# Products as pairs of half-row matmuls between the score blocks, in an attention and gated-FFN kernel

## The chip, the cores and the metric

The kernel runs on one core of one Trainium2 chip. The metric is the device time of one execution in microseconds (us). The engines go by short names: PE is TensorE (PEld its weight loads), DVE is VectorE, ACT is ScalarE, POOL is GpSimd, SP is SyncE, whose queue issues most DMAs here.

## The reference

x has 2048 rows of 576. With xn = layernorm(x), everything in float32:

```
q, k, v = xn @ wqkv                     # 32 heads of 18
s = softmax(q k^T * 18^-0.5) v @ wo     # attention over all 2048 rows
g = silu( (gelu(xn @ w_gate) * (xn @ w_up)) @ w_down )     # w_gate, w_up 576 x 4608, w_down 4608 x 576
out = x + s * g
```

## The kernel before, in words

**Operands.** A float32 product of projections is made of three fp16 ones: each operand is split into a high and a low half, and hi*hi, hi*lo and lo*hi are added up in PSUM. XHT holds the transposed high halves of xn (four tiles of 128 rows, and a fifth, XT, with the last 64 rows' high halves above their low halves), XL the low ones. A gate, up, q or k product of 128 output rows and 512 columns of the sequence is `mm_wx`: 14 matmuls, each with 128 rows of contraction and 512 columns. A down tile (`dn`) is two half tiles of 288 columns, six matmuls each. The v and output products go through `mm_xw`, 14 matmuls of 288 columns.

**Scores.** Heads go in 16 pairs; the two heads of a pair stand on rows 0 to 63 and 64 to 127. `qk1` (L940) makes scores of queries by keys on 54 rows, and VectorE takes their row maximum (L943, tile PM); one call is two matmuls, one for each half of the rows. `qk2` (L980) makes the transposed scores with the maximum already subtracted, on 56 rows, and ScalarE takes exp (L986, tile P). `pv` (L1002) multiplies P with V in float32 on four tiles of 32 columns; each float32 matmul is two records in the trace, 16 in a call for both steps' P tiles.

**PSUM.** Eight banks: s1 for qk1 (two banks), s2 for qk2 (two), pv (one), and three rotating m tiles (`MTile`) for all projections. In the main loop s1 and s2 have one buffer each, so a qk1 waits for the maximum of the qk1 before, a qk2 for the exp of the qk2 before.

**Order.** All instructions are issued in an order written out by hand; each engine's queue works in that order. The main loop runs over pairs p and 32 steps s. A step issues qk2 for pair p, qk1 for pair p+1, some filler, qk2 and qk1 again, and then filler (odd s) or `pv` for two steps (even s). Filler is a generator (`filler_gen`) that yields one matmul at a time, with its time: q/k of the later heads (units j), the 18 chunks of the gated FFN (units c: gate, up, a down tile between them), and at last the output product. `fill(amount)` takes matmuls from it until the amount, left time over left steps, is used up.

`subtick` is the clock of all else: each call advances `defer` (work put off by a number of ticks: evacuations, the gelu chain on POOL and ACT, stores) and takes one piece from `bg`, the queue of weight preparations (`prep`: load, maxima L170 and L175, scales L210 to L227, high halves on ACT, remainders L239 and L250 on DVE). A step has four ticks.

**Stages.** Up to 180 us: load, layernorm, transposes, q/k of the first heads, v, and qk1 of pair 0 with v and j1 as filler. From 180 to 2603 us: pairs 0 to 14. Then pair 15 (which has no qk1 to run ahead), the output products, and the end.

Of the kernel before, what the change touches and what calls it, by code (L numbers as in the profile page):

```python
# [12 lines left out]
F32 = mybir.dt.float32  # L13
# [11 lines left out]
NJ = 5  # L25
# [6 lines left out]
FILL_PRO = 0.92  # L32
LATE = 14
V_PLAN = {8: 2, 9: 2, 10: 1, 12: 1, 13: 4, 14: 2, 15: 3, 16: 3, 17: 1}
T_WX, T_XW = 0.216, 0.123
# [3 lines left out]
T_V = NT * 2 * 14 * T_XW  # L39
T_J = NB * 2 * 14 * T_WX  # L40
T_C = NB * 4 * 14 * T_WX + NT * 12 * T_XW
# [26 lines left out]
def kernel(ctx: ExitStack, tc: tile.TileContext, x, wqkv, wo, w_gate, w_up, w_down, out):  # L68
# [33 lines left out]
    m_pend = []  # L102

    class MTile:


        def __init__(self, shape, dt, readers):
            until(lambda: len(m_pend) < 3 or m_pend[-3] == 0)
            self.i = i = len(m_pend)
            m_pend.append(readers)  # L110
            self.t = ps.tile(shape, dt, tag="m", name=f"m{i}", bufs=3)

        def done(self):
            m_pend[self.i] -= 1
# [16 lines left out]
    def prep(name, parts, n, down=None, urgent=False, free=None, dfree=None):  # L131
# [47 lines left out]
        def par():  # L179
# [7 lines left out]
            if urgent:  # L187

                mt = ps.tile([P, 512], F32, tag="pv", name=f"mp_{name}")
# [3 lines left out]
                mt = ps.tile([P, 512], F32, tag="pv", name=f"mb_{name}")  # L193
# [96 lines left out]
    def mm_wx(o, w, i, c0, c1, s0, s1, end=None):  # L290

        k = 0
        for t in range(4):
            for (lw, xx) in ((w.hi, XH), (w.hi, XL), (w.lo, XH)):
                nc.tensor.matmul(o, lw[:, t, i, c0:c1], xx[:, t, s0:s1], start=(k == 0), stop=False)  # L295
                k += 1
                yield 0.216
        nc.tensor.matmul(o, w.hi[:, 4, i, c0:c1], XT[:, s0:s1], start=False, stop=False)  # L298
        yield 0.216
        nc.tensor.matmul(o, w.lo[:, 4, i, c0:c1], XT[:, s0:s1], start=False, stop=True)  # L300
        if end is not None:
            end()
        yield 0.216
# [64 lines left out]
    def proj_j_sb(w, j, part, sb):  # L368
        n = w.n
        mt = MTile([P, 512], F32, 2)  # L370
        yield from mm_wx(
            mt.t[0:n, :], w, part, 0, n, 512 * sb, 512 * sb + 512,
            lambda: evac_j(j, part, sb, mt, n),
        )

# [12 lines left out]
    def unit_j(w, j):  # L388
        open_j(w, j)
        for sb in range(NB):  # L390
            for part in (1, 0):
                yield from proj_j_sb(w, j, part, sb)
# [10 lines left out]
    def unit_v(w):  # L403
        nc.vector.tensor_copy(EV, w.E[:, 0:1])
        for st in range(NT):
# [3 lines left out]
            for hf in range(2):  # L409
                mt = MTile([P, 512], F32, 1)  # L410
# [24 lines left out]
    def gu(w, c, sb, ft):  # L435
        s0 = 512 * sb
        cs = slice(P * ft, P * ft + P)
        st = {}
        gp = nc.gpsimd
        g = MTile([P, 512], F32, 1)  # L440

        def copy():
# [3 lines left out]
            st["t0"] = defer.now  # L446
            defer.at(defer.now + 1, cubic)
            defer.at(defer.now + 4, th)
            defer.at(defer.now + 5, one)
# [6 lines left out]

        def th():
            nc.scalar.activation(st["t"], st["t"], AF.Tanh, scale=GK)  # L458
# [3 lines left out]

        yield from mm_wx(g.t, w, 0, cs.start, cs.stop, s0, s0 + 512, copy)
        yield from dn_unit()

        u = MTile([P, 512], F32, 1)

        def mul():
            st["v"] = wp.tile([P, 512], F32, tag="gv", name=f"gv_{c}_{sb}_{ft}")
            nc.vector.scalar_tensor_tensor(  # L470
                st["v"], u.t, w.uE[:, 1:2], st["g"], op0=ALU.mult, op1=ALU.mult
            )
            u.done()
            t = max(defer.now + 1, st["t0"] + 6)
            defer.at(t, hp)
            defer.at(t + 2, hhi)
            defer.at(t + 3, hlo)
# [4 lines left out]
        def hhi():  # L482
            if ft == 0:
                hs = hstate[c, sb] = W()
                hs.n = 0
# [4 lines left out]
        def hlo():  # L490
            hs = hstate[c, sb]
            gp.tensor_tensor(hs.lo[:, ft], st["v"], hs.hi[:, ft], op=ALU.subtract)  # L492
            hs.n += 1

        yield from mm_wx(u.t, w, 1, cs.start, cs.stop, s0, s0 + 512, mul)
        yield from dn_unit()
# [4 lines left out]
    def dn(w, c, sb, si):  # L501

        until(lambda: (c, sb) in hstate and hstate[c, sb].n == 2)
# [3 lines left out]
        for hf in range(2):  # L507
            ms = slice(288 * hf, 288 * hf + 288)
            mt = MTile([P, 512], F32, 1)
            yy = Y[0][:, st, ms]  # L510
            k = 0
            for ft in range(2):
                for a, b in ((hs.hi, w.dhi), (hs.hi, w.dlo), (hs.lo, w.dhi)):
                    nc.tensor.matmul(  # L514
                        mt.t[:, 0:288], a[:, ft, sl], b[:, ft, ms], start=(k == 0), stop=(k == 5)
                    )
                    k += 1
                    if k < 6:
                        yield T_XW
            if c == 0:  # L520
                nc.vector.tensor_scalar(yy, mt.t[:, 0:288], w.c, None, op0=ALU.mult)
            else:
                nc.vector.scalar_tensor_tensor(yy, mt.t[:, 0:288], w.c, yy, op0=ALU.mult, op1=ALU.add)  # L523
            mt.done()
            yield T_XW
        dndone[c] += 1
        if c == NCH - 1 and si == 3:
            queue_gate(sb)

    def dn_unit(lag=5):  # L530

        if len(dnq) > lag:
            yield from dnq.popleft()

    def unit_c(w, c):
        if c == 0:
            Y[0] = cp.tile([P, NT, D], F32, tag="xy", name="y")
        for sb in range(NB):
            dnq.extend(dn(w, c, sb, si) for si in range(4))
            for ft in range(2):  # L540
                yield from gu(w, c, sb, ft)
        if c == NCH - 1:
            while dnq:
                yield from dn_unit(0)
# [67 lines left out]
    obdone = [0, 0]  # L612
    last_o = {}
# [24 lines left out]
    def unit_out(qc, whole):  # L638
# [13 lines left out]
        for si in range(2):  # L652
# [8 lines left out]
            for hf in range(2):  # L661
                ms = slice(288 * hf, 288 * hf + 288)
                mt = MTile([P, 512], F32, 1)
# [518 lines left out]
```

## Time and profile before

| | us |
|---|---|
| median of three runs | 2792.64 (2792.05 to 2792.81) |
| the profiled execution, its own time | 2790.57 |
| its span, first to last instruction | 2788.7 |
| busy PE, PEld | 2708.0, 1100.4 |
| busy DVE, ACT, POOL | 2026.7, 1596.9, 926.9 |
| mean granted TensorE clock | 0.993 of full |

Matmuls are pipelined and their rows overlap: a row's length is not the time that it takes of PE. The distance from one start to the next is. The rows named m are projections (L295, L298, L300 in `mm_wx`; L514 down; L310 to L315 in `mm_xw`), s the scores.

### The profile page before, as it was taken

To read this page: it belongs to the slowest core of one execution; us is meant where nothing else is said; L and a number is where in the kernel's file an instruction comes from. 1 tells how busy PE (TensorE), PEld (TensorE's weight loads), DVE (VectorE), ACT (ScalarE), POOL (GpSimd) and SP (SyncE) were. 2 spreads that over 40 slices of the span, in tenths; PEclk is the share of its full clock that TensorE was granted. 3 is DMA by queue.
4 is the path that set the end of the run, shared out by engine and by line. 5 is a ranking of instruction groups with operands and counts; after the bars stand their busy time and mean duration, and the time that the engine had idled before them with its cause. 6 is when DMAs were issued, how large, how long until landed. Compare 5 with 4: busy or idle time off the path is not lost.

```text
span 2788.7 us, 44258 instructions
## 1 busy us (share of the span) xinstructions
PE 2708.0 (97%) x17736; PEld 1100.4 (39%) x17736; DVE 2026.7 (73%) x2703; ACT 1596.9 (57%) x1948; POOL 926.9 (33%) x976
## 2 busy tenths in 40 slices
PE   6989999999999999999999999999999999999998
PEld 6533333333333333333333333333333333333354
DVE  7787767767777777777777777777777777777354
ACT  5136556655665556665656565666655555656652
POOL 4113331333223331343333333333333333333301
PEclk9999999999999999999999999999999999999999
DMA  4330102102030202102011110101021001010113
GB/s 137 125 103 13 48 13 85 31 8 52 20 80 15 49 13 75 39 3 54 7 49 31 30 39 7 48 9 48 14 48 27 21 21 36 20 34 9 37 52 128
DMA packets 133258, 117.36 MB, mean 42 GB/s; under 512 B 60096, under 2 KB 112472, under 8 KB 133052
## 3 DMA queue, kind: packets, MB, share of 16 engines
q1 hardware_dynamic: 128828, 103.28, 13.6%
q0 software_dynamic: 3072, 8.90, 0.9%
q8 instruction: 138, 2.26, 0.4%
q10 hardware_dynamic: 1152, 2.36, 0.2%
q14 instruction: 68, 0.56, 0.1%
HBM read 84.89 MB, written 29.61 MB: 41 GB/s over the span
## 4 chain that ended last, share of the span: by engine, by line
PE 82%; DVE 13%; issue 2%; DMA 2%; ACT 1%; SPq 0%; POOL 0%; ACTq 0%; DVEq 0%; POOLq 0%
PE m L295 28%; PE pv L1002 14%; PE m L514 14%; PE s L980 10%; PE s L940 8%; DVE PM L943 5%; PE m L310 3%; PE m L298 2%; PE m L300 2%; DVE m_c L170 1%; DVE gv L470 1%; DVE y L523 1%; DVE wlo_c L239 1%; DVE dlo_c L250 0%; DMA KD<-evh 0%
## 5 line engine op out<-in xcount | busy, mean ns | idle before, releaser
L943 DVE TENSOR_REDUCE PM<-s 128x2 f32<-128x1024 f32 x1024 | 1249.4, 1223 | 571.2 <-PE s L940 565.2
L986 ACT ACTIVATE P<-s,etab 128x1024 f32<-128x1024 f32 x896 | 997.0, 1113 | 843.5 <-PE s L980 834.9
L1002 PE MATMUL pv<-P,VT 128*32 128x512 f32 x4096 | 492.5, 598 | 0.0
L295 PE MATMUL m<-XHT,whi_c 128*128 128x512 f16 x1152 | 438.7, 381 | 6.1 <-DVE gv L470 6.0
L295 PE MATMUL m<-XHT,wlo_c 128*128 128x512 f16 x1152 | 439.1, 381 | 1.8 <-DVE wlo_c L239 1.8
L295 PE MATMUL m<-XL,whi_c 128*128 128x512 f16 x1152 | 439.1, 381 | 0.0
L940 PE MATMUL s<-KT,QT 54*128 54x512 f16 x2048 | 390.4, 379 | 31.2 <-DVE PM L943 26.3
L980 PE MATMUL s<-QT,KT 56*128 56x512 f16 x2048 | 400.4, 387 | 8.8 <-ACT P L986 8.7
L453 POOL TENSOR_TENSOR tw<-gs 128x512 f32<-128x512 f32 x144 | 150.5, 1045 | 665.7 <-ACT gs L444 665.6
L480 POOL TENSOR_TENSOR gv<-gv,tw 128x512 f32<-128x512 f32 x144 | 186.2, 1293 | 465.8 <-DVE gv L470 434.6
L514 PE MATMUL m<-dhi_c,hlo 128*128 128x288 f16 x1152 | 330.3, 287 | 0.8 <-POOL hlo L492 0.8
L514 PE MATMUL m<-dhi_c,hhi 128*128 128x288 f16 x1152 | 330.5, 287 | 0.2 <-ACT hhi L488 0.2
L514 PE MATMUL m<-dlo_c,hhi 128*128 128x288 f16 x1152 | 330.3, 287 | 0.0
L295 PEld LDWEIGHTS <-whi_c 128*128 128x128 f16 x2304 | 215.8, 98 | 272.2 <-issue 103.0
L523 DVE SCALAR_TENSOR_TENSOR y<-m,c_c,y 128x288 f32<-128x288 f32 x544 | 266.5, 509 | 43.0 <-PE m L514 41.1
L980 PEld LDWEIGHTS <-KT 56*128 56x128 f16 x2048 | 99.0, 93 | 494.8 <-issue 493.1
L514 PEld LDWEIGHTS <-hhi 128*128 128x128 f16 x2304 | 217.7, 98 | 161.1 <-issue 70.7
L492 POOL TENSOR_TENSOR hlo<-gv,hhi 128x512 f16<-128x512 f32 x144 | 167.3, 1162 | 252.9 <-ACT hhi L488 252.9
L1002 PEld LDWEIGHTS pv<-P,VT 128*32 128x32 f32 x4096 | 106.8, 109 | 256.0 <-issue 256.0
L455 POOL TENSOR_TENSOR tw<-tw,gs 128x512 f32<-128x512 f32 x144 | 185.0, 1285 | 12.0
L295 PEld LDWEIGHTS <-wlo_c 128*128 128x128 f16 x1152 | 112.7, 98 | 163.2 <-issue 57.4
L461 POOL TENSOR_SCALAR tw<-tw 128x512 f32<-128x512 f32 x144 | 90.2, 626 | 202.8 <-ACT tw L458 200.8
(172 smaller groups left out, 2710.9 us busy)
## 6 DMA issues: line engine op xcount, KB each, us to landing
draw_c<-in_B_w_down SPq DMA_DIRECT2D x18, 576.0 KB
raw_c<-in_B_w_gate SPq DMA_DIRECT2D x18, 512.0 KB
raw_c<-in_B_w_up SPq DMA_DIRECT2D x18, 512.0 KB
obr<-rd SPq DMA_DIRECT2D x30, 256.0 KB
KT<-KD SPq DMA_DIRECT2D x32, 224.0 KB
QT<-QD SPq DMA_DIRECT2D x32, 216.0 KB
VS<-vst POOLq DMA_DIRECT2D x16, 304.0 KB, 3.0
VT<-VS SPq DMA_DIRECT2D x16, 304.0 KB
```

The lines of the kernel that those rows point to most:

```text
L295: nc.tensor.matmul(o, lw[:, t, i, c0:c1], xx[:, t, s0:s1], start=(k == 0), stop=False)
L453: gp.tensor_tensor(st["t"], st["g"], st["g"], op=ALU.mult)
L455: gp.tensor_tensor(st["t"], st["t"], st["g"], op=ALU.mult)
L480: gp.tensor_tensor(st["v"], st["v"], st["t"], op=ALU.mult)
L492: gp.tensor_tensor(hs.lo[:, ft], st["v"], hs.hi[:, ft], op=ALU.subtract)
L514: nc.tensor.matmul(mt.t[:, 0:288], a[:, ft, sl], b[:, ft, ms], start=(k == 0), stop=(k == 5))
L523: nc.vector.scalar_tensor_tensor(yy, mt.t[:, 0:288], w.c, yy, op0=ALU.mult, op1=ALU.add)
L940: nc.tensor.matmul(s1[:, h], QT[p][r, P * qt:P * qt + P], KT[p][r, 512 * kb:512 * kb + 512], start=True, stop=True)
L943: nc.vector.tensor_reduce(PM[p][:, :, qt, kb:kb + 1], s1, op=ALU.max, axis=AX.X)
L980: nc.tensor.matmul(s2[:, h], KT[p][r, P * kt:P * kt + P], QT[p][r, 512 * qb:512 * qb + 512], start=True, stop=True)
L986: nc.scalar.activation(pt, s2, AF.Exp, scale=ETAB[j0])
L1002: nc.tensor.matmul(o[qd:qd + 32, :], VT[p][:, c0:c0 + 32], pt[:, h], start=(kt == 0), stop=(kt == NT - 1), skip_group_check=True,)
```

## The change

1. Gate and up of one 128-row tile (or k and q of one block of 512) become a `Pair`: 54 matmuls of 64 rows in place of 28 of 128. In stage 0, product a runs on rows 0 to 63 of its operands and b on rows 64 to 127, one of each alternately, into two PSUM tiles; in stage 1 they change halves. A stage has 14 slots of two matmuls (the last of one). A stage 1 starts only once a score tile that was issued after the end of stage 0 has been used again.
2. The m ring of three becomes three tiles with names: ma and mb for a pair, mc for down (and ma as well where no pair is open).
3. Filler by amount is gone from the main loop for these products. A pair runs either fast (14 slots in an odd step, 10 and 4 in the even one) or slow (6 and 2, or 5 and 4 where no down waits; the even step ends the stage), as the count of stages is behind a straight line over the steps or not.
4. Down half tiles wait in a queue and are issued at the end of a step: one at an odd step, one or two ahead of P times V and at times one behind it at an even one.
5. Gate and up evacuate together: copy of gate at the end of the pair, product with up two ticks later, the rest of the chain at fixed ticks.
6. In the prologue, pairs stand between the score blocks and v alone is filler; j1's weights are prepared ahead of the score loop. The last chunk takes its column blocks in the order 2, 3, 0, 1. The output products start when all downs are done.

```
+    def half_terms(w, i, cs, xs, half):
+        r = slice(64 * half, 64 * half + 64)
+        terms = []
+        for t in range(4):
+            for lw, xx in ((w.hi, XH), (w.hi, XL), (w.lo, XH)):
+                terms.append((lw[r, t, i, cs], xx[r, t, xs]))
+        terms.append((w.hi[r, 4, i, cs], XT[r, xs]))
+        if half == 0:
+            terms.append((w.lo[r, 4, i, cs], XT[r, xs]))
+        return terms
...
+            if self.stage == 0:
+                self.q = [(a, half_terms(w, ia, cs, xs, 0)), (b, half_terms(w, ib, cs, xs, 1))]
+            else:
+                self.q = [(b, half_terms(w, ib, cs, xs, 0)), (a, half_terms(w, ia, cs, xs, 1))]
...
+        def end(g, u):
             st["g"] = wp.tile([P, 512], F32, tag="gs", name=f"gs_{c}_{sb}_{ft}")
             nc.scalar.activation(st["g"], g.t, AF.Copy, scale=w.uE[:, 0:1])
             g.done()
+            t = defer.now
+            defer.at(t + 1, cubic)
+            defer.at(t + 2, lambda: mul(u))
+            defer.at(t + 5, th)
+            defer.at(t + 6, one)
+            defer.at(t + 8, hp)
+            defer.at(t + 10, hhi)
+            defer.at(t + 11, hlo)
+            if ft == 1:
+                defer.at(t + 13, lambda: dnq.extend(
+                    (w, c, sb, si, hf) for si in range(4) for hf in range(2)
+                ))
...
+    def g_run(n, new=True):
+        while n > 0 and not gs.over:
+            if not gs.open:
+                if gs.pair is not None and seen[0] <= gs.end:
+                    return
+                if gs.pair is None:
+                    if not new:
+                        return
+                    gs.pair = next(gstream, None)
...
+                gs.pair.begin()
+                gs.open = True
+            n -= 1
+            if gs.pair.slot():
...
+        preps[1], pieces = prep(*order[1][1], urgent=True, mtag="s2")
...
-    for item in range(0, 64, 2):
-        qk1(0, item)
-        qk1(0, item + 1)
-        fills(2, FILL_PRO)
+    for k in range(32):
+        qk1(0, 2 * k)
+        g_run((3, 2, 2, 0)[k % 4])
+        qk1(0, 2 * k + 1)
+        fills(2, 0.68)
+        g_run((2, 2, 3, 0)[k % 4])
...
+            odd = s % 2 == 1
+            if odd and not gs.open and gs.pair is None:
+                want = g0 + (G_ALL - LATE - g0) * (2 * NT * p + s) / (2.0 * NT * (NPAIR - 1))
+                fast = gs.n < want and len(dnq) > 0
+            if fast:
+                n1, n2 = (14, 0) if odd else (10, 4)
+            elif odd:
+                n1, n2 = (6, 2) if dnq else (5, 4)
             else:
+                n1, n2 = 9, 0
...
             pa = qk2(p, 2 * qh, kt)
             if kp < NPAIR:
                 qk1(kp, next(items))
-            fills(2, amt)
+            subtick()
+            g_run(n1, odd)
...
             pb = qk2(p, 2 * qh + 1, kt)
             if kp < NPAIR:
                 qk1(kp, next(items))
+            g_run(n2, odd)
...
-            if s % 2 == 0:
+            if odd:
+                down("mc")
+                if gs.over:
+                    down("ma")
+            else:
+                if down("mc") and gs.pair is None:
+                    down("ma")
                 for u in pend[:-1]:
                     pv(*u)
                 pend = pend[-1:]
-                fills(2, 0.0)
-            else:
-                fills(2, amt)
+                if len(dnq) > 8:
+                    down("mc")
```

Here gs.n counts stages, gs.open says that one is running, and dnq holds the half tiles of down that are free to run.

More of the change, by code (lines that the diff above doesn't have):

```diff
@@ L445, in copy @@
             g.done()
[L446 to L449, printed above, removed]
+            t = defer.now
[10 more added lines that the diff above has]
+                ))
+        end.readers = 1
         def cubic():
@@ L473, in mul, with th, one @@
             u.done()
[L474 to L477, printed above, removed]
+        def th():
+            nc.scalar.activation(st["t"], st["t"], AF.Tanh, scale=GK)
+        def one():
+            gp.tensor_scalar(st["t"], st["t"], 1.0, 1.0, op0=ALU.mult, op1=ALU.add)
         def hp():
@@ L1086 @@
     while vdone[0] < NT or not mdone.get(0):
[L1087 removed]
+        fills(1, 1.0)
+    for _ in filler[0]:
+        pass
     def last_gen():
```

251 lines of the change are left out of this document (140 added, 111 removed).

## The prediction

> **What bounds the kernel now.** I read the page's head, the busy times by stage, one stretch of the timeline, and last the waits of the engines that the changed order will press on.
>
> ```profile
> span 2788.7 us, 44258 instructions
> PE 2708.0 (97%) x17736; PEld 1100.4 (39%) x17736; DVE 2026.7 (73%) x2703; ACT 1596.9 (57%) x1948; POOL 926.9 (33%) x976
> ```
> ```profile
> 0.00:180.10 180.10, 149.23 (x1295) 102.69 (x1295) 147.91 (x249) 58.00 (x114) 44.09 (x84) 0.98 0.39 122
> 180.10:2602.70 2422.60, 2387.79 (x15260) 912.47 (x15260) 1798.61 (x2323) 1449.88 (x1738) 850.00 (x857) 1.00 0.13 33
> 2602.70:2788.70 186.00, 170.99 (x1184) 85.25 (x1183) 80.14 (x133) 89.06 (x96) 32.77 (x36) 0.96 0.25 81
> ```
>
> (Stretch, length, then PE, PEld, DVE, ACT and POOL busy with counts, granted clock, DMA share, GB/s.) The middle row is the loop over pairs 0 to 14: 2422.6 us, 15 x 16 = 240 double steps (an even and an odd s) of 10.09 us. PE's 97% hides a loss, because a matmul's row runs on while the next one streams. The starts show it:
>
> ```profile
> 1285.03 0.38 PE L295 MATMUL m<-XL,whi_c 128*128 128x512 f16 x1
> 1285.24 0.38 PE L295 MATMUL m<-XHT,wlo_c 128*128 128x512 f16 x1
> 1285.55 0.39 PE L980 MATMUL s<-QT,KT 56*128 56x512 f16 x2
> 1285.57 0.10 PEld L940 LDWEIGHTS <-QT 54*128 54x128 f16 x2
> 1285.78 0.38 PE L940 MATMUL s<-KT,QT 54*128 54x512 f16 x2
> 1286.09 0.39 PE L295 MATMUL m<-XHT,whi_c 128*128 128x512 f16 x1
> 1286.20 1.23 DVE L943 TENSOR_REDUCE PM<-s 128x2 f32<-128x1024 f32 x1 [0.78 <-PE s L940]
> 1286.32 0.38 PE L295 MATMUL m<-XL,whi_c 128*128 128x512 f16 x1
> 1286.54 0.38 PE L295 MATMUL m<-XHT,wlo_c 128*128 128x512 f16 x1
> ```
>
> Full matmuls of 512 columns start 0.215 us apart. Two score matmuls, one on each half of the rows, start together and count as one. Going from full to halves takes 0.31 (1285.24 to 1285.55), the next start 0.23, the way back 0.31, and the next 0.23: 1.08 in place of 4 x 0.215, so **0.108 us for one change of shape**. A double step now has three stretches of filler between score blocks and one of P times V, eight changes: 240 x 8 x 0.108 = 207 us of the loop. That is what the change goes for.
>
> P times V stands on 32-column tiles. From it to halves, and to full matmuls (in the tail), it is the same:
>
> ```profile
> 1291.23 1.92 PE L1002 MATMUL pv<-P,VT 128*32 128x512 f32 x16
> 1293.08 0.39 PE L980 MATMUL s<-QT,KT 56*128 56x512 f16 x2
> ...
> 2760.60 1.92 PE L1002 MATMUL pv<-P,VT 128*32 128x512 f32 x16
> 2762.45 0.30 PE L310 MATMUL m<-whi_wo,ohl 128*128 128x288 f16 x1
> ```
>
> 1.85 us to the next start both times. So down next to P times V is a change too, not a free neighbour.
>
> **The change part by part. Changes of shape.** I followed the new loop with the diff's numbers (slots 14,0 and 10,4 for a fast pair; 6,2 or 5,4, then 9 for a slow one; eight downs released 13 ticks after a chunk's last product; four ticks a step). The prologue's g_run calls sum to 14 slots in every four rounds, eight stages, so four of the 160 pairs are done; 156 remain for 480 steps. A fast pair takes two steps, a slow one four: 72 fast, 84 slow. That makes 72 fast double steps and 168 slow ones. Scores and pairs have one shape, so only downs and P times V cost. Even steps: a down ahead of P times V in 211 of 240 (three changes), none in the rest (two). Odd steps: a down in 214 (two), none in 26. Sum 633 + 58 + 428 = 1119 against 1920: 801 x 0.108 = **-87 us**.
>
> **The pairs.** 28 full matmuls become 54 half ones in 28 slots, on two PSUM tiles. No row here shows a long run of half pairs. Bounds: 0.215 a slot (as full matmuls) and 0.227 (L980's pair to L940's, the second after a change); for 4354 slots in the loop, 0 to +48 us. Full matmuls too need 0.23 at that place (1286.09 to 1286.32) and 0.215 after it, so I take **0**. The exchange of halves itself waits for nothing: a stage starts only when a score tile issued behind the last one has been reused.
>
> A rule that speaks against this stands in the Trainium skill, "TensorE: Matmul & The Clock Gate", Part 3: a weight load runs beside a matmul only if it goes to other rows. By it the loop would take some 430 us more. The trace disagrees: L940's loads start at 1285.57, on the rows of L980's matmuls of 1285.55, and its matmuls start 0.23 after those.
>
> **The score blocks come closer together.** This is the price. qk1 keeps one buffer, s1, freed by the maximum on VectorE:
>
> ```profile
> 1502.80 1.21 DVE L943 TENSOR_REDUCE PM<-s 128x2 f32<-128x1024 f32 x1
> 1503.93 0.68 DVE L1034 TENSOR_TENSOR osb<-osb,obr 128x512 f32<-128x512 f32 x1
> ...
> 1504.07 0.39 PE L940 MATMUL s<-KT,QT 54*128 54x512 f16 x2 [0.56 <-DVE PM L943]
> ```
>
> PM's start to the qk1 it frees is 1.27; a qk1 to its PM 0.42 (1285.78 to 1286.20): no two qk1 can be closer than **1.69 us**. Now they stand 2.3 to 2.6 apart (1285.78 and 1288.28 below) and rarely wait:
>
> ```profile
> 1288.05 0.39 PE L980 MATMUL s<-QT,KT 56*128 56x512 f16 x2
> 1288.28 0.38 PE L940 MATMUL s<-KT,QT 54*128 54x512 f16 x2
> 1288.59 0.30 PE L514 MATMUL m<-dlo_c,hhi 128*128 128x288 f16 x1
> 1288.72 0.29 PE L514 MATMUL m<-dhi_c,hlo 128*128 128x288 f16 x1
> 1288.84 0.29 PE L514 MATMUL m<-dhi_c,hhi 128*128 128x288 f16 x1
> ```
> ```profile
> L940 PE MATMUL s<-KT,QT 54*128 54x512 f16 x1912 | 365.5, 378 | 24.5 <-DVE PM L943 23.0 <-DVE mx_wo L181 0.3
> L295 PE MATMUL m<-XHT,whi_c 128*128 128x512 f16 x1125 | 428.4, 381 | 6.1 <-DVE gv L470 6.0
> ```
>
> In the new order the distance is one slot for qk1, the filler slots, and one for qk2; a down between adds 6 x 0.123 and two changes, 0.95. Slow with 6 slots: 8 x 0.215 = 1.72, just enough. Slow with 5 (no downs waiting when the step began; 81 odd and 81 even steps in my count): 1.51, a wait of 0.18. In 26 of those odd steps no down arrives either, and the second half, 6 x 0.215 = 1.29, waits 0.40. Fast odd, second half (no slot, one down): 0.43 + 0.95 = 1.38, a wait of 0.31, 72 times. Together 29 + 10 + 22 = **+62 us**, rounded up. exp on s2 asks for less, 1.65 (the L980 rows below), so it adds nothing here.
>
> On top come VectorE's other jobs, which stand between two maxima in its queue:
>
> ```profile
> L523 DVE SCALAR_TENSOR_TENSOR y<-m,c_c,y 128x288 f32<-128x288 f32 x520 | 254.1, 509 | 16.7 <-PE m L514 14.7
> L239 DVE SCALAR_TENSOR_TENSOR wlo_c<-raw_c,s_c,whi_c 128x512 f16<-128x512 f32 x90 | 74.3, 832 | 0.0
> L170 DVE TENSOR_REDUCE m_c<-raw_c 128x1 f32<-128x512 f32 x85 | 55.9, 675 | 2.9 <-DMA raw_c<-in_B_w_up 2.6 <-issue 0.2
> L250 DVE SCALAR_TENSOR_TENSOR dlo_c<-draw_c,s_c,dhi_c 128x576 f16<-128x576 f32 x36 | 30.6, 873 | 0.0
> L175 DVE TENSOR_REDUCE m_c<-draw_c 128x1 f32<-128x576 f32 x34 | 25.0, 741 | 0.0
> ```
>
> A maximum leaves 1.72 - 1.13 = 0.59 us of a tight distance (1502.80 to 1503.93), less 0.5 where a down is taken up. A chunk's preparation, 185.8 us in these last four rows, puts two amax jobs into a distance (1.35) or one remainder (0.83). 336 of 480 steps are slow, and three of four distances there are tight: 0.525 x 185.8 = 97 us meet them. Of amax's share, 42, about two thirds stick out (1.35 against 0.59, or against 0.1); of the remainders' 55, some 0.4: 27 + 22, and about 10 for the nine small scale jobs in one tick. That is 59, against 33 that qk1 waits now (24.5 in its row, and 48 waits whose rows hide another 0.17 each behind the overlap). I take **+25**; bounds 0, if they fall as softly as now, and +72, if all 97 stand. Where a job already holds a qk1 back, the planned wait is not paid again: **-10**, an estimate.
>
> **Buffers.** Three rotating m tiles become ma, mb, mc. The pair needs both ma and mb free; its evacuations are a copy on ScalarE at once and the product on VectorE two ticks later, and the next pair starts behind a P times V stretch of 1.85 (fast) or a step later (slow). So L295's wait for gv, 6.0, goes: **-6**; at worst it stays. Behind a waiting qk1 on PE stand the slots and P times V, and nobody else is starved: GpSimd, 850 of 2422.6 us busy, has ticks to spare between cubic and th.
>
> **Moved work.** The stage view of the loop for L295 alone, and for L514 alone:
>
> ```profile
> 180.10:2602.70 2422.60, 913.90 (x3664) 1.00 0.13 33
> ...
> 180.10:2602.70 2422.60, 487.23 (x3312) 1.00 0.13 33
> ```
>
> L295 holds twelve of a product's fourteen matmuls, so 4275 full ones are in the loop now; my count puts 4354 slots there, and 563 half downs of six, 3378. The 79 and the 66 come from the last pair: 17 + 8 = +25. The last pair loses them, but its order is held by exp:
>
> ```profile
> 2608.35 0.39 PE L980 MATMUL s<-QT,KT 56*128 56x512 f16 x2 [0.43 <-ACT P L986]
> 2610.00 0.39 PE L980 MATMUL s<-QT,KT 56*128 56x512 f16 x2 [0.51 <-ACT P L986]
> 2611.66 0.39 PE L980 MATMUL s<-QT,KT 56*128 56x512 f16 x2 [0.30 <-ACT P L986]
> 2613.84 0.39 PE L980 MATMUL s<-QT,KT 56*128 56x512 f16 x2
> ...
> 2758.84 0.39 PE L980 MATMUL s<-QT,KT 56*128 56x512 f16 x2
> ```
>
> 1.65 without P times V, 2.18 with it. It lasts 156 now (2602.70 to 2758.84). New: seven steps until the last downs are done, about 4.4 each, then 25 with 52.6 us of output (T_LAST), 2.1 a step: 1.65, 2.18 + 1.05, 1.65, 1.65 for two steps, 4.1 each. 31 + 104 = 135: -21. Net **+4**.
>
> **Prologue.** The same matmuls; j1's preparation moves ahead of the score loop, and its four loads stand on SP's queue ahead of the last q/k stores, which load_qk waits for. Between nothing and 8 us (the first stage moves 122 GB/s; 0.65 MB more is 5): **+2**, since v products cover most of it.
>
> Sum: -87 + 0 + 62 + 25 - 10 - 6 + 4 + 2 = -10. The profiled execution took 2790.57 (span 2788.7); 2780.6. The median of the runs, 2792.64, stands 2.1 above it, so **2782**.
>
> **The rivals.** What can be told from no change is about 0.2%, 2787 to 2798.
> A, the forecast: VectorE's round trip takes back most of what the changes of shape give. 2765 to 2800.
> B, the waits stay small: downs nearly always wait, so slow steps run with 6 slots and only the fast odd ones wait, and the jobs fall as softly as now. -87 + 22 - 6 + 4 + 2 = -65: 2728. For it: VectorE is 74% busy in the loop, and fast steps and each P times V leave it 1 to 2 us. Against: 62 is arithmetic on two latencies.
> C, slower: s1 as the bound. Every job of VectorE in a tight distance holds PE for all its length, since with one s1 nothing absorbs it: +72 in place of +25, no overlap: 2839. It decides once over 35 us more than my 25 stick out. For it: the wait of 0.56 at 1504.07 came behind jobs in a distance that was not even tight.
> D: a slot takes 0.227: +48, 2830.
> E, the change doesn't do what it says: score blocks of 54 and 56 rows and pairs of 64 count as different shapes. Some five more changes a double step: 240 x 5 x 0.108 = +130, 2912. Against it: L980 has 56 rows, L940 54, and they follow each other at 0.23.
> F: a slot waits for its half's weights, 0.10 as L940's loads take: 4354 x 0.10 = +435, 3218. Against it: those loads ran while L980's matmuls streamed.
>
> **How the numbers follow.** A 0.40, B 0.28, C 0.25, D 0.05, E 0.01, F 0.01. The rule on weight loads named above is what F would be; its chance is what one pair of score blocks leaves open. Of A, 0.22 lies under 2787, 0.14 within the band, 0.04 over it. Faster 0.22 + 0.28 = 0.50; same 0.14; slower 0.36. Cases of both signs hold much, so beside A's own 2765 to 2800 the range is 2710 to 2850: it leaves out the lower end of B, the upper of C, E and F.
>
> **What would show it.** In the new trace: half pairs 0.215 apart, with no 0.31 where they meet a score block; the row of L940 with an idle time of some 80 to 110 us put down to PM, against 24.5; qk1 starts at 1.69 in rows; pairs of P times V and down with 0.22 to 0.23 between them; the last pair near 135 us. A slot of 0.225 or more, loads that wait for matmuls, or a loop over pairs 0 to 14 under 2370 or over 2470 us would make me wrong.

## The result and the profile after

The changed kernel takes 2890.3 us (median of 4 runs, 2887.0 to 2892.4) against 2792.7 of the kernel before in the same session: a ratio of **1.035, interval 1.033 to 1.037**, 98 us slower. Its profiled execution took 2892.4, the span 2890.6. The page's first lines, and the busy time by stage (bounds at the first qk2 of pair 0 and of pair 15; columns as in the prediction):

```profile
span 2890.6 us, 52567 instructions
PE 2697.1 (93%) x21900; PEld 1233.0 (43%) x21900; DVE 2025.9 (70%) x2703; ACT 1587.0 (55%) x1948; POOL 931.8 (32%) x976
```
```profile
0.00:203.10 203.10, 154.24 (x1405) 103.73 (x1405) 151.50 (x252) 59.50 (x117) 44.22 (x84) 0.94 0.36 113
203.10:2716.10 2513.00, 2395.06 (x19446) 1055.91 (x19447) 1803.00 (x2336) 1444.08 (x1746) 870.50 (x873) 0.99 0.12 32
2716.10:2890.60 174.50, 147.78 (x1049) 73.39 (x1048) 71.40 (x116) 83.40 (x86) 17.11 (x19) 0.94 0.26 85
```

| stage | before | after | difference | forecast |
|---|---|---|---|---|
| up to the loop | 180.1 | 203.1 | +23.0 | +2 |
| loop, pairs 0 to 14 | 2422.6 | 2513.0 | +90.4 | +9 |
| pair 15 | 156.1 | 144.4 | -11.7 | -21 |
| the end | 29.9 | 30.0 | 0 | 0 |

VectorE, ScalarE and GpSimd do the same work (2026, 1587 and 932 us against 2027, 1597 and 927); only the order is another. First, what came as planned: the timeline of PE, across a slow step.

```profile
1282.24 0.38 PE L1014 MATMUL s<-KT,QT 54*128 54x512 f16 x2
1282.46 0.38 PE L342 MATMUL ma_t<-XHT,whi_c 64*128 64x512 f16 x1
1282.46 0.38 PE L342 MATMUL mb_t<-XHT,whi_c 64*128 64x512 f16 x1
1282.68 0.37 PE L342 MATMUL ma_t<-XL,whi_c 64*128 64x512 f16 x1
...
1283.32 0.38 PE L342 MATMUL ma_t<-XHT,wlo_c 64*128 64x512 f16 x1
1283.67 0.39 PE L1054 MATMUL s<-QT,KT 56*128 56x512 f16 x2
1283.94 0.39 PE L1014 MATMUL s<-KT,QT 54*128 54x512 f16 x2
...
1284.89 0.29 PE L560 MATMUL mc_t<-dhi_c,hlo 128*128 128x288 f16 x1
1285.11 1.92 PE L1076 MATMUL pv<-P,VT 128*32 128x512 f32 x16
1286.96 0.39 PE L1054 MATMUL s<-QT,KT 56*128 56x512 f16 x2
```

A score block runs into a pair's slots after 0.22 (1282.24 to 1282.46), the two halves start together, and slots are 0.22 apart, 0.215 to 0.216 in the median of all the loop's slots. L1014 is the old L940 (qk1), L1054 the old L980 (qk2), L342 a slot, L560 down, L1076 the old L1002. The weights of the next slot are loaded while both halves still stream (these two rows come from another step; the matmul on mb starts at 1313.52 too):

```profile
1313.52 0.37 PE L342 MATMUL ma_t<-XL,whi_c 64*128 64x512 f16 x1
1313.52 0.10 PEld L342 LDWEIGHTS <-wlo_c 64*128 64x128 f16 x2
```

At 1283.67 is the trouble: the last slot began 0.35 earlier, and qk2 should have followed after 0.22. The waits of PE show where such gaps end (what was waited for: us in total, times, longest; a row's length hides another 0.17 of each). First the loop before, then the loop now, then the whole run now, with which the rows of the experiments below are to be compared:

```profile
PE s L940 <- DVE PM L943: 23.0, 41, 2.0
PE s L980 <- ACT P L986: 1.2, 1, 1.2
```
```profile
PE s L1014 <- DVE PM L1017: 48.6, 64, 2.0
PE s L1054 <- ACT P L1060: 31.4, 91, 2.2
```
```profile
PE s L1014 <- DVE PM L1017: 50.6, 67, 2.0
PE s L1054 <- ACT P L1060: 47.4, 110, 5.6
PE s L1054 <- DMA QT<-md: 8.1, 3, 4.2
PE ma_t L342 <- ACT whi_j L237: 5.7, 1, 5.7
```

By the starts (each PE start against the usual distance of the same two operations) 565 starts of qk1 and qk2 in the loop come late, for 171 us in all; before, they were some 37 us late. The granted clock takes a small part: it is 0.99 in the loop against 1.00, and starts at about twice their usual distance add some 12 us against 5 (slots at 208.00 and 208.43 are 0.43 apart, where the granted clock is 0.50). What lies ahead of a late qk1 (rows of GpSimd, of weight loads and of DMA issues, and some of PE and ScalarE, are left out):

```profile
1312.48 0.74 DVE L240 SCALAR_TENSOR_TENSOR wlo_c<-raw_c,s_c,whi_c 128x512 f16<-128x512 f32 x1
...
1313.08 0.38 PE L1014 MATMUL s<-KT,QT 54*128 54x512 f16 x2
1313.14 0.51 DVE L567 SCALAR_TENSOR_TENSOR y<-mc_t,c_c,y 128x288 f32<-128x288 f32 x1
...
1313.57 0.74 DVE L240 SCALAR_TENSOR_TENSOR wlo_c<-raw_c,s_c,whi_c 128x512 f16<-128x512 f32 x1
...
1314.23 1.22 DVE L1017 TENSOR_REDUCE PM<-s 128x2 f32<-128x1024 f32 x1
1314.51 0.39 PE L1054 MATMUL s<-QT,KT 56*128 56x512 f16 x2
1315.00 1.11 ACT L1060 ACTIVATE P<-s,etab 128x1024 f32<-128x1024 f32 x1 [0.54 <-PE s L1054]
1315.50 0.39 PE L1014 MATMUL s<-KT,QT 54*128 54x512 f16 x2 [0.59 <-DVE PM L1017]
```

The scores of 1313.08 could have been reduced from 13.50 on. But the sum of a down half tile (y) and a remainder of the next chunk's weights (wlo) stand ahead in VectorE's queue, and the maximum starts at 14.23. The next qk1 could start at 14.73; it starts at 15.50, behind a wait of 0.77. The distance held five slots, 1.51 us; with 2.5 us the same two jobs would have gone unnoticed.

### The profile page after: what moved, and what is told of

It is laid out like the page before. It is cut to its first block, busy times and chain, and to the rows that moved or that the text cites. A ratio compares the mean times of both kernels' runs of the same rounds, so it can differ in the third digit from the quotient of the medians.

```text
span 2890.6 us, 52567 instructions
## 1 busy us (share of the span) xinstructions
PE 2697.1 (93%) x21900; PEld 1233.0 (43%) x21900; DVE 2025.9 (70%) x2703; ACT 1587.0 (55%) x1948; POOL 931.8 (32%) x976
## 5 line engine op out<-in xcount | busy, mean ns | idle before, releaser
L342 PE MATMUL ma_t<-XHT,whi_c 64*128 64x512 f16 x1440 | 541.8, 376 | 1.2 <-DVE y L565 1.1
L342 PE MATMUL mb_t<-XHT,whi_c 64*128 64x512 f16 x1440 | 541.7, 376 | 0.0
L1076 PE MATMUL pv<-P,VT 128*32 128x512 f32 x4096 | 498.4, 605 | 2.3 <-DMA VT<-VS 2.3
L1054 PE MATMUL s<-QT,KT 56*128 56x512 f16 x2048 | 426.3, 384 | 67.6 <-ACT P L1060 47.4
L342 PE MATMUL mb_t<-XHT,wlo_c 64*128 64x512 f16 x1296 | 487.4, 376 | 0.0
L342 PE MATMUL ma_t<-XHT,wlo_c 64*128 64x512 f16 x1296 | 487.2, 376 | 0.0
L1014 PE MATMUL s<-KT,QT 54*128 54x512 f16 x2048 | 415.4, 380 | 53.4 <-DVE PM L1017 50.6
L342 PE MATMUL ma_t<-XL,whi_c 64*128 64x512 f16 x1152 | 432.4, 375 | 0.0
L342 PE MATMUL mb_t<-XL,whi_c 64*128 64x512 f16 x1152 | 432.4, 375 | 0.0
L342 PEld LDWEIGHTS <-whi_c 64*128 64x128 f16 x5184 | 268.3, 94 | 276.6 <-issue 4.8
L1054 PEld LDWEIGHTS <-KT 56*128 56x128 f16 x2048 | 150.6, 93 | 451.9 <-issue 377.6
L560 PEld LDWEIGHTS <-hhi 128*128 128x128 f16 x2304 | 191.8, 98 | 212.2 <-issue 170.5
L560 PE MATMUL mc_t<-dhi_c,hhi 128*128 128x288 f16 x864 | 253.0, 293 | 10.0 <-DVE rms L1037 10.0
L560 PE MATMUL mc_t<-dhi_c,hlo 128*128 128x288 f16 x864 | 248.9, 288 | 0.0
L560 PE MATMUL mc_t<-dlo_c,hhi 128*128 128x288 f16 x864 | 248.9, 288 | 0.0
L1014 PEld LDWEIGHTS <-QT 54*128 54x128 f16 x2048 | 155.9, 94 | 153.6 <-issue 115.4
```

The source lines that it names most:

```text
L342: nc.tensor.matmul(o, lw, xx, start=self.stage == 0 and self.k == 0, stop=self.stage == 1 and self.k == len(terms) - 1, skip_group_check=True,
L560: nc.tensor.matmul(mt.t[:, 0:288], a[:, ft, sl], b[:, ft, ms], start=(k == 0), stop=(k == 5))
L1014: nc.tensor.matmul(s1[:, h], QT[p][r, P * qt:P * qt + P], KT[p][r, 512 * kb:512 * kb + 512], start=True, stop=True)
L1054: nc.tensor.matmul(s2[:, h], KT[p][r, P * kt:P * kt + P], QT[p][r, 512 * qb:512 * qb + 512], start=True, stop=True)
L1076: nc.tensor.matmul(o[qd:qd + 32, :], VT[p][:, c0:c0 + 32], pt[:, h], start=(kt == 0), stop=(kt == NT - 1), skip_group_check=True,)
```

## The experiments

All medians, with the ratio to the kernel before (2790 to 2793 in each session). The two columns on the loop come from one profiled execution each; the executions of one kernel spread by up to 9 us, so a few us between two loops say nothing.

| kernel | us | ratio, interval | loop starts | loop |
|---|---|---|---|---|
| the change | 2890.3 | 1.035 [1.033, 1.037] | 203.1 | 2513.0 |
| a_half_exp | 2859.2 | 1.024 [1.022, 1.025] | 201.4 | 2491.4 |
| a_half_max | 2807.1 | 1.005 [1.003, 1.007] | 194.4 | 2438.1 |
| a_half_both | 2736.3 | 0.980 [0.978, 0.981] | 195.1 | 2376.8 |
| b_half_both | 2746.5 | 0.983 [0.982, 0.985] | 178.9 | 2384.7 |
| a_full_rows | 2939.4 | 1.053 [1.052, 1.055] | 198.8 | 2562.5 |
| a_old_prologue | 2872.8 | 1.029 [1.028, 1.031] | 183.8 | 2512.3 |
| a_even2 | 2968.8 | 1.064 [1.062, 1.065] | 200.8 | 2583.7 |
| a_pool_lows | 2971.1 | 1.064 [1.063, 1.066] | 201.7 | 2591.3 |
| a_level | 3000.3 | 1.074 [1.072, 1.075] | 183.6 | 2636.2 |
| a_no_prep | 2843.5 | 1.018 [1.017, 1.020] | 201.2 | 2468.4 |
| a_half_exp_no_prep | 2814.6 | 1.008 [1.006, 1.009] | 200.1 | 2449.2 |
| a_half_max_no_prep | 2790.4 | 0.999 [0.998, 1.000] | 191.7 | 2421.1 |
| a_jobs | 2836.5 | 1.017 [1.015, 1.018] | 184.6 | 2474.9 |
| a_jobs2 | 2811.3 | 1.008 [1.006, 1.009] | 188.7 | 2452.2 |
| a_jobs3 | 2829.6 | 1.014 [1.012, 1.015] | 184.5 | 2469.2 |
| a_jobs3p | 2835.8 | 1.016 [1.014, 1.017] | 184.0 | 2479.0 |

**Which wait: the maximum, exp, or both?** ScalarE has other jobs too, from the page's groups (busy us, mean ns of one):

```profile
L491 ACT ACTIVATE gs<-ma_t,uE_c 128x512 f32<-128x512 f32 x144 | 98.6, 685 | 9.8 <-PE ma_t L342 3.2
L535 ACT ACTIVATE hhi<-gv 128x512 f16<-128x512 f32 x144 | 89.9, 624 | 0.0
L522 ACT ACTIVATE tw<-tw 128x512 f32<-128x512 f32 x144 | 89.3, 620 | 0.0
L237 ACT ACTIVATE whi_c<-raw_c,s_c 128x512 f16<-128x512 f32 x90 | 62.3, 713 | 0.0
```

Halving either operation shortens its round trip and leaves PE's order as it is. It also empties the engine's queue for that time, so it takes off both the round trip and a part of the waiting behind other jobs.

```
a_half_exp:  scalar.activation(pt[:, :, 0:256], s2[:, :, 0:256], AF.Exp, ...)   # P times V reads these columns twice
a_half_max:  vector.tensor_reduce(PM[...], s1[:, :, 0:256], ...)                # scores scaled down by 4
a_half_both, b_half_both:  both, in the changed kernel and in the kernel before
```

> The changed kernel, with exp on half of the columns alone (P times V reads that half for both heads; the other half of the attention weights is left out). Matmuls, order and VectorE's work stay. Theory W (PE waits at the score blocks for both round trips, exp on s2 and the maximum on s1): the loop over pairs 0 to 14, 2513 now, loses 40 to 70 us, the wait of qk2 for exp goes nearly to zero and qk1's wait for the maximum grows a little: 2820 to 2850 in all. Rival V (VectorE alone, as the prediction had it: exp adds nothing): under 15 us. Rival M (the half-row matmuls themselves cost the time): under 15 us.

> The changed kernel, with the row maximum over half of each block's columns (and the exponent's scale divided by four, so that nothing overflows). Theory W: the loop loses 40 to 80 us, qk1's wait for the maximum nearly goes, qk2's wait for exp stays or grows: 2810 to 2850. Rival V (VectorE alone): the loop loses all of what it gained in waits, 120 to 150 us. Rival M: under 15 us.

> Both halvings together. Theory W: both round trips are far under the distance of score blocks, so the loop falls to its matmuls and changes of shape, 2178 + 125 + some 20 to 40 of other waits: 2325 to 2345, 2690 to 2730 in all. Rival M (half-row matmuls cost more than 0.215 a slot in runs): loop over 2450.

> The kernel before with both halvings, the control. Theory W: its score blocks stand 2.3 to 2.6 apart, over both round trips, so only its 55 us of waits can go: the loop, 2422.6, loses 30 to 55 us. Then the loop of the changed kernel with both halvings is 30 to 70 us below this one: that is what the removed changes of shape are worth. If both kernels lose the same, the waits are no matter of the new order.

PE's waits for the two, first with half exps, then with half maxima, then with both, and in the kernel before with both:

```profile
PE s L1014 <- DVE PM L1017: 79.8, 151, 1.9
PE s L1054 <- ACT P L1060: 15.3, 18, 5.2
```
```profile
PE s L1054 <- ACT P L1060: 45.5, 118, 5.6
PE s L1014 <- DVE PM L1017: 8.4, 12, 1.0
```
```profile
PE s L1014 <- DVE PM L1017: 19.8, 29, 1.0
PE s L1054 <- ACT P L1060: 13.9, 16, 5.2
```
```profile
PE s L940 <- DVE PM L943: 4.8, 6, 1.9
```

Without exp's wait, the maximum's takes its place: its row goes from 50.6 to 79.8, and the loop gains only 21.6. Without the maximum's the loop gains 74.9, and exp's row stays (47.4 to 45.5). Without both it gains 136.2. So neither round trip is the bound alone, and exp's, which the prediction put at nothing, is worth 61.3 once the maximum is out of the way (2438.1 to 2376.8). a_half_exp's 21.6 lies between its theories (40 to 70, and under 15), a_half_max's 74.9 in the range of theory W.

With both halved the change's loop is 7.9 us shorter than that of the kernel before (2376.8 against 2384.7); the same halving is worth 37.9 there. Of the 90.4 us that the loop lost, **98.3 (136.2 - 37.9) are what the two halvings take away, the two round trips with what queues behind them**, and all the rest together is a gain of 7.9. Theory W had 30 to 70 for that gain, and a loop of 2325 to 2345 with both halved: both missed. The halvings do not end the waits: by the starts, qk1 and qk2 still come some 44 us late in a_half_both, against 9 in b_half_both.

**Is the pairing itself at fault?** The same order, with the slots as full matmuls.

```
-            self.q = [(a, half_terms(w, ia, cs, xs, 0)), (b, half_terms(w, ib, cs, xs, 1))]   # and stage 1
+            self.q = [((a, b)[self.stage], full_terms(w, (ia, ib)[self.stage], cs, xs))]
```

> The changed kernel, with each pair's 28 slots as full matmuls of 128 rows again (14 for one product, then 14 for the other, on the same two tiles and at the same places): the order, the downs and all waits stay, the pairing goes. Theory W (the pairing gives what it should, and the loss is in the distances of the score blocks): every change of shape between a score block and a stage comes back; 4354 slots lie in some 640 stretches of the loop, so up to 1280 changes x 0.108 = 138 us, of which a good part falls into distances in which PE waits anyway (242 us of waits in the loop of the change): +30 to +90 over the change, 2920 to 2980. Rival M (half-row matmuls have a price of their own, a slower slot or their weight loads, and the changes of shape saved are less than that): at or below the change, 2890 or less.

```profile
198.80:2761.30 2562.50, 2462.51 (x15403) 947.01 (x15404) 1800.91 (x2336) 1444.50 (x1746) 870.46 (x873) 0.99 0.12 31
```

49.5 us more in the loop, in the range of theory W. The half-row pairs are worth that much here, less than the 138 of all changes of shape, since many of these fall into distances where PE waits anyway (by the starts, qk1 and qk2 come some 50 us less late than in the change). The fault is not in them.

**The prologue.**

```
-    for k in range(32): qk1(0, 2k); g_run((3, 2, 2, 0)[k % 4]); qk1(0, 2k + 1); fills(2, 0.68); g_run((2, 2, 3, 0)[k % 4])
+    for k in range(32): qk1(0, 2k); qk1(0, 2k + 1); fills(2, 0.92)      # filler: v, then j1 in full rows
```

> The changed kernel with the prologue of before: v products and then the two products of the second unit of q and k as full-row filler behind the score blocks, no pairs there, and the second unit's weights not prepared ahead. Theory W: the loop starts at 180 to 184 us in place of 203 and is else as it was (2513 +-10 from there on): 2867 to 2873. A rival: the weights' preparation and the downs, which start 20 us earlier, run into the same due times, so that the loop gets longer by what the prologue gets shorter: 2880 to 2892.

The loop starts at 183.8 and is as long as in the change (2512.3): 19.3 of the prologue's 23.0 us come back, 17.5 of the whole, as theory W had it. In the change the first pair waited 5.7 us for its high halves (row `ma_t <- ACT whi_j` above); and in the order of before, j1's matmuls ran after the last qk1 of pair 0 and covered the way of pair 0's maxima to qk2, which now stands bare: PE was busy for all 11.8 us of it, and is now for 3.4 of 12.3 us (190.8 to 203.1).

**Is it the spread of the work?** Two orders with the same slots. a_even2: 0 7, 7 0, 7 7, 0 4, 10 0, 10 4 slots in six steps. a_level: P times V alone, downs behind 5, 5 and 4 slots, two downs in one gap.

```
-                n1, n2 = (14, 0) if odd else (10, 4)      # fast; slow: (6, 2) or (5, 4), then 9
+            ph = 2 * ((32 * p + s - 1) % 6)
+            n1, n2 = SLOT6[ph], SLOT6[ph + 1]
a_even2:  SLOT6 = (0, 7, 7, 0, 7, 7, 0, 4, 10, 0, 10, 4)
a_level:  SLOT6 = (7, 7, 0, 0, 5, 5, 4, 0, 14, 0, 14, 0)
```

> The changed kernel with the same slots spread evenly: instead of fast steps (14 slots, 0, 10, 4) and slow ones (6, 2 or 5, 4, then 9), a fixed pattern over six steps: 0 7, 7 0, 7 7, 0 7, 4 10, 0 10, 4, with the downs put in the distances that have no slots. So no distance of a score block is without work of at least 1.4 us, and most are at 7 slots (1.93 us) or a down. Theory W (waits for the two round trips of 1.69 and 1.65 us in short distances): of the 242 us of waits in the loop, 60 to 100 go; 2790 to 2830. Rival V (VectorE's jobs between two maxima set the waits, wherever the slots are): within 30 of the change, 2860 to 2890.

> The changed kernel with the prologue of before and with level distances: P times V alone in its distance (2.4 us), stages of 14 slots as 7 and 7, as 5, 5 and 4 with a down behind each, and twice as 14, and two downs together in the other gaps (2.1 us). In its order 156 distances are at 1.93 us and 24 are empty (no down ready), the others at 2.1 to 3.3; in the change 450 of 960 are under 1.82 while P times V stands in distances of 3.2 to 4.9. It has 1284 changes of shape in the loop, 166 more than the change (+18 us). Theory W (a short distance loses, and a long one gives nothing back): 240 us of waits in the loop become 60 to 100, the loop is 2390 to 2430 and the whole 2740 to 2785, under the kernel before. Rival (the waits are there because two queues are loaded, wherever the work stands): the loop keeps 180 or more of waits, 2830 or more.

Both missed by far. PE's waits, a_even2 and then a_level (whose line numbers are two lower):

```profile
PE s L1054 <- ACT P L1060: 122.4, 276, 4.6
PE s L1014 <- DVE PM L1017: 24.3, 55, 1.5
```
```profile
PE s L1052 <- ACT P L1058: 66.3, 86, 4.6
PE ma_t L342 <- DVE y L567: 54.8, 66, 1.8
PE s L1012 <- DVE PM L1015: 41.6, 53, 3.5
PE mc_t L560 <- DVE y L567: 22.1, 22, 1.4
```

a_even2's expectation miscounted: 250 of its 960 distances hold one down or nothing (1.38 us at most), and most P times V stand in distances of 4 to 5. In a_level the distances are longer, but a stage of 14 follows the gap in which the second down took ma, and waits for its y, which stands on VectorE behind the other down's y and mostly behind the product with up (gv): 54.8 us, and 22.1 for mc, 77 us of waits that no theory had named. The granted clock is 0.98 in this loop, and starts at about twice their usual distance add some 40 us, against 10 in a_old_prologue. Its rows for exp and the maximum still come to 108, with few distances under 1.9 us. So "long distances cure it" fell in this form. Why exp waits so long in a_level was not taken apart.

**Are the other jobs the cause?** Chunks 9 to 17 use the weights of chunk 8; then the same with half exps, and with half maxima.

```
+            if kind[0] == "c" and kind[1] > 8:
+                preps[i] = preps[i - 1]
+                return
```

> The changed kernel, in which chunks 9 to 17 use the weights of chunk 8: their loads, maxima, high halves and remainders are left out (some 93 us of VectorE's work and 9 x 7 jobs of ScalarE), so their products are not those of the reference. The matmuls and their order are the same. Theory J (jobs that stand between two maxima or two exps make most of what the bare round trip doesn't): the waits of the loop's second half, 37 us of qk1 and 43 of qk2, become some 15 and 25, and the whole is 25 to 50 shorter, 2840 to 2865. Rival (the bare round trips are it): 10 or less, 2880 or more.

> The kernel with exp on half of its columns (2859), in which chunks 9 to 17 use the weights of chunk 8 as well (not prepared, so not the reference's products; half of the exps are left out). Only the maximum can hold PE here: 149 us of qk1's waits, of which the bare distances explain 63. Theory J: of the 68 us in the second half some 30 are left, 2815 to 2835. Rival (the round trip itself is longer than 1.69): 2850 or more.

> The kernel with the maximum on half of its columns (2807), in which chunks 9 to 17 use the weights of chunk 8 as well (not prepared, so not the reference's products; half of each row is left out of the maximum). Only exp can hold PE: 97 us of qk2's waits, 42 of them in the second half. Theory J: high halves that stand between two exps make a part of these; 10 to 25 come back, 2782 to 2797. Rival (exp's waits are bare distances, as its shortest distance of 1.65 has nothing to give): 5 or less, 2802 or more.

46.8, 44.7 and 16.8 us come off: what theory J gave, the second 0.4 us beyond its range. The maximum's row in the first of them, and in the second (79.8 before):

```profile
PE s L1017 <- DVE PM L1020: 22.1, 32, 2.0
```
```profile
PE s L1017 <- DVE PM L1020: 48.8, 121, 1.9
```

The matmuls and their order are unchanged, so the distances are too. What went are jobs between two maxima and between two exps (and the loads of these weights).

**Would another engine take the jobs?**

```
-            nc.vector.scalar_tensor_tensor(w.lo[:, t], w.raw[:, t], w.s[:, 0:1], w.hi[:, t], op0=ALU.mult, op1=ALU.subtract)
+            nc.gpsimd.tensor_scalar(w.raw[:, t], w.raw[:, t], w.s[:, 0:1], None, op0=ALU.mult)
+            nc.gpsimd.tensor_tensor(w.lo[:, t], w.raw[:, t], w.hi[:, t], op=ALU.subtract)
```

> The changed kernel with the remainders of the chunks' weights (126 jobs of 0.83 to 0.87 us, 105 us in all) on GpSimd in place of VectorE, two operations each. Theory W: some of the waits for the maximum (78 us) were these jobs standing between two maxima; a third to a half of the 105 us come back, and exp's waits stay: -20 to -40, 2850 to 2870. Rival: the distances themselves are too short, jobs or not: within 10 of the change, 2880 to 2900.

Slower by 81. ScalarE's waits, GpSimd's first new operation in the page's groups, and PE's wait:

```profile
ACT hhi L538 <- POOL gv L531: 87.2, 25, 6.7
```
```profile
L245 POOL TENSOR_SCALAR raw_c<-raw_c,s_c 128x512 f32<-128x512 f32 x90 | 142.4, 1582 | 128.2 <-ACT whi_c L237 117.1 <-PE s L1017 10.9
```
```profile
PE s L1057 <- ACT P L1063: 112.8, 130, 10.9
PE s L1017 <- DVE PM L1020: 30.2, 35, 2.0
```

The maximum's row falls by 20, as hoped. But GpSimd now works on the remainders when the gelu chain's product is due, ScalarE waits for that product with its conversion (hhi; no such wait in the change), and exp is queued behind: exp's row goes from 47.4 to 112.8, its longest wait from 5.6 to 10.9. Some 20 of the 78 us that the loop grew are the clock's: it is 0.98 there, and starts at about twice their usual distance add some 32 us in place of 12.

**Is it their place?** On a_old_prologue: the pieces of preparation go only into long distances. a_jobs2: the second down ahead of P times V only while more than two half tiles wait. a_jobs3: the tanh earlier as well. a_jobs3p: also one of two P times V units in the gap of fast steps.

```
+            k1 = int(n1 >= 10 or gs.over)                              # pieces a tick, first half of a step
+            k2 = 0 if odd and not gs.over else 1 + (n2 > 2)            # second half
-            subtick()
+            subtick(k1)                                                # and subtick(k2)
a_jobs2:   -  if down("mc") and gs.pair is None:
           +  if ... down("mc") and gs.pair is None and (len(dnq) > 2 or not nxt):
a_jobs3:   -  defer.at(t + 5, th)
           +  defer.at(t + (4 if fast else 3), th)
a_jobs3p:  +  if n1 == 14 and len(pend) > 1: pv(*pend.pop(0))
```

> The changed kernel with the prologue of before (2872.8), in which the pieces of the weights' preparation (maxima and remainders on VectorE, high halves on ScalarE) are issued only in long distances: those with P times V (up to two a distance in slow steps, four in fast ones), with 14 or with 10 slots. Nothing is left out and the matmuls keep their order. Theory J (a job costs where the distance is short, and nothing in a long one): of the 47 us that half of the preparation cost, so some 90 for all of it, half or more come back: 2790 to 2830. Rival (the queues' load decides, wherever the jobs stand; a_even2 and a_level speak for it): 2860 to 2885.

> As a_jobs, and the second down ahead of P times V is issued only while more than two half tiles wait, so that the store of half tiles runs dry less often: by its order 76 distances of 4 or 5 slots in place of 188 (and 280 of 6 in place of 174), with 19 more changes of shape (2 us). The bare loss below 1.70 us goes from 67 to 44 in its order. Theory J: 15 to 30 under a_jobs. Rival: a distance of 6 slots (1.72) loses as much as one of 5, since both leave no room for a job: within 8 of a_jobs.

> As a_jobs2, with the tanh of the gate issued one or two ticks earlier, so that it stands in the distance of P times V (slow steps) or in a long one (fast steps) and no longer between the two exps of an odd step. In the trace of a_jobs2 the tanh stands ahead of 15 to 25 us of qk2's waits. Theory J: 10 to 20 under a_jobs2, 2791 to 2801. Rival (ScalarE then stands behind GpSimd's cubic, and exp behind it): 0 or slower, 2811 to 2830.

> As a_jobs3, and in fast steps one of the two P times V units (8 matmul records, 0.86 us) is issued in the distance that holds nothing but a down (72 times, 1.38 us of work against 1.65 and 1.70): 71 more changes of shape (8 us) for 25 us of waits. Theory W: 10 to 20 under a_jobs3, 2771 to 2791, at or under the kernel before. Rival: P of the step before is not ready so early, and the unit waits for exp: no gain, or slower by up to 20.

a_jobs: 36.3 us under a_old_prologue, 6 short of the range that theory J gave, and with nothing left out. The maximum's row there and in a_old_prologue:

```profile
PE s L1015 <- DVE PM L1018: 22.3, 41, 2.1
```
```profile
PE s L1012 <- DVE PM L1015: 53.7, 71, 2.0
```

a_jobs2 is another 25.2 lower: theory J's 15 to 30. Its 2811.3 is the lowest of the variants that leave nothing out, and still 0.8% over the kernel before. a_jobs3 is 18 slower than a_jobs2, and ScalarE's waits say why:

```profile
ACT tw L525 <- POOL tw L515: 166.6, 82, 2.9
```

The tanh now waits for GpSimd's cubic (a_jobs2 has no such wait), with exp behind it: its rival's mechanism, at the rival's price. a_jobs3p: the bare gap is filled, and 6 us more is the result, where its theory had 10 to 20 less; the starts show exp's waits smaller by 15 and the maximum's larger by 8, with 71 changes of shape more. No version found beats the kernel before.

## Why the prediction was wrong, by its own steps

It forecast 2782 with 2710 to 2850, and 2890 came.

- **Changes of shape, -87: right in kind.** By the starts there are 1131 (about a dozen of them around transposes, which the sum did not count) in place of 1933, and the time over the pitch that they cost goes from 184.7 to 111.4: -73. That is 0.096 and 0.099 a change, not 0.108: the prediction's 0.108 holds the next start's 0.23, and qk2 to qk1 still takes 0.226 in the new order.
- **Slots, 0: right.** 0.215 to 0.216 each; neither D, E nor F. The page's row for L342 on ma has 1.2 us of idle time in 1440 matmuls, so the wait for gv is gone too. The trace decides against the Trainium skill's rule that the prediction named ("TensorE: Matmul & The Clock Gate", Part 3): weight loads of 64 rows ran beside matmuls on the same 64 rows all through the loop (the two rows of 1313.52 above), 8397 loads of L342 that were busy for 457.9 us, and of 3646 distances from slot to slot 10 are over 0.222, 9 of them where the granted clock is halved.
- **qk1's planned waits, +62: right.** In a_half_exp, where exp doesn't interfere, the 162 distances of five slots, 1.51 us of work, stand at 1.70 from the lowest quarter to the median, and so do the 72 of the fast steps (1.71, by the start of a block's second half). The planned distances are all there in the count (162, 72 and 26 of the three kinds), 62 us by the prediction's own prices.
- **VectorE's other jobs, +25 with bounds 0 to 72, less 10: the step that failed first.** By the starts qk1 waits 149 us in a_half_exp; less the planned 62 that is 87, where the prediction had 59. Less the 35 us that qk1 waited before, it is +52 in place of +25 less 10 (+35 if the start of a block's second half is counted): inside the bounds, but over the value taken. Half of the preparation alone is worth 45 to 47 (a_no_prep, a_half_exp_no_prep). The prediction took averages: a maximum "leaves 1.72 - 1.13 = 0.59 us of a tight distance". But tight distances come three in a row, and jobs at each tick, so what sticks out of one is not taken up by the next; this reading of the order is argued, and a_jobs, which moves the jobs alone, supports it. Case C had this mechanism and its price (+72, no overlap).
- **exp, 0: the second.** The prediction compared exp's 1.65 with the maximum's 1.69 ("asks for less, 1.65") and stopped there. It did not do for ScalarE what it did for VectorE: gs, hhi, tanh and the high halves (0.62 to 0.71 us each, rows above) stand between exps, and a distance of 1.72 has 0.07 to give. Worth 21.6 beside the maximum's waits and 61.3 without them.
- **Prologue, +2 with 0 to 8: the third.** +23.0; 19.3 of it came back with the old one. The sum counted the loads on SP's queue, not that j1's matmuls covered the way of pair 0's maxima.
- **Moved work, +4.** 4354 slots and 3378 downs were counted in the loop as predicted. The last pair lost 11.7, not 21; with both operations halved it took 135.1, and 154.3 in the kernel before so halved.

By the starts the waits at the score blocks grew by 134 us (171 less 37), where the sum had 62 + 25 - 10 = 77. Of the 108 us between forecast and result these are some 57, the prologue 21, the changes of shape 14 and the last pair 9; the few left over are of the size of the clock's part.

"VectorE's round trip takes back most of what the changes of shape give" was so the right place with the wrong size; both round trips took back 98, more than the changes of shape gave, and no case held the prologue. Its marks: the loop came out over 2470, and the idle time of qk1's row, set at 80 to 110, was 50.6, because exp's waits took the place of a part of it (79.8 in a_half_exp).

## What to carry to other kernels

A stage that hands one buffer to another engine has a shortest distance, and what counts is that distance plus the jobs that stand in that engine's queue, for every engine in the handover, not for the busiest alone. When work is moved between such blocks, list the distances before and after: here one long and three short lost more (98 us) than the saved changes of shape gave (73), as a long one gave nothing back. If the short ones must stay, put the other jobs into the long ones; that gave 36 us here without touching the matmuls. Levelling the distances was no cure in the two orders tried: other waits came in their place, and what an order without them would give stays open.

## What the hardware showed unexpectedly

- Two matmul streams on the two 64-row halves keep 0.215 to 0.216 us a slot of two in the median of 4354 slots, mixed with score blocks; only where the granted clock is 0.50 do they take 0.43.
- Moving 126 jobs took 88 us from VectorE's loop time (1803.0 to 1715.4) and put 363 us on GpSimd's (870.5 to 1233.5): a tensor_scalar of 128x512 with its factor from a tile took 1.58 us (L245 above), while GpSimd's tensor_scalar of the same shape with constants (on tw, in the same run) took 0.62.
